# A Fourier filter feeding a squared-ReLU FFN: the last quarter of one batch's first transform moved into the first FFN group

## The chip, the cores and the metric

The kernel runs on one core of a Trainium2 chip. The metric is the device time of one execution in microseconds (us), as the median of several runs. The profile is of one further execution, and its times count from the start of that execution's span.

## The reference, cut to what matters

```python
X = np.fft.rfft(x, axis=1)                       # x: 8 batches, 3008 tokens, 256 features
Y = X * (filt_r + 1j * filt_i)[None, :, :]       # one complex factor per frequency and feature
y = np.fft.irfft(Y, n=3008, axis=1).astype(np.float32)
x = y.reshape(24064, 256)
h = np.maximum(x @ w_in, 0.0)                    # 256 -> 2048
return (h * h @ w_out).astype(np.float32)        # 2048 -> 256
```

## The kernel before, in words

The Fourier filter is four matmul stages per batch, since 3008 = 64 x 47. Stage A (`unit_a`, or `chunk_a` in the prologue) transforms over one factor and gives a tile u, which goes through DRAM to be turned (`write_u` stores a quarter of it to dU, L344; `read_u` loads the whole batch as ut, L436). Stage B (`unit_b`, L445) transforms over the other factor, and VectorE multiplies its result by the filter (L453, L460, L461, L467). Stage P (`unit_p`, L496) begins the inverse and stores to dZ; `read_z` (L514) loads it as four tiles zt; stage Y (`unit_y`, L532) finishes the inverse into yt, the FFN's input, in 16 units of 4 small matmuls.

The FFN takes groups of 512 tokens. A group has 8 slots. `ffn_g1(g, s)` (L562) makes 256 of the 2048 hidden features: 4 matmuls of 512 columns into a tile psH, which ScalarE empties with a ReLU (L566); `ffn_sq` squares the half-precision result on VectorE (L570). One group later, `ffn_g2` (L579) multiplies by W_out: 8 matmuls of 256 columns per slot, emptied by ScalarE (L590) and stored. psH has two buffers.

The order of the work is written out by hand. The main loop at L728 goes through the slots: g1 of this group, the planned work of place 0, g2 of the group before, the planned work of place 1, the output of the group before, the squaring. `fft_plan(b)` (L610) says in which slot and place each unit of batch b's filter stands. For batch 1 plan slot 0 is slot 0 of the main loop, so plan slots 0 to 7 are FFN group 0, which has no g2 of a group before it, and slots 8 to 15 are group 1. Every engine runs its instructions in this order.

Before the loop stands a prologue: the filter of batch 0 (but for Y units 4 to 15), and three quarters of stage A of batch 1: chunks 0, 2, 1 in this order (L712), stored by three `write_u` (L715). The last quarter (`unit_a` 12 to 15, chunk 3) stands in the plan, two units each in slots 8 and 9. In the plan stand too the Y units 4 to 15 of batch 0, and four casts of W_out to half precision (`cast_wout`, L333, on VectorE, slots 4, 5, 7, 7). W_out arrives in two halves by DMA (L328) into a tile of the pool p_h2, which is the buffer that group 1's hidden tile takes next.

Two small pools matter here. psF, a PSUM tile of one bank with two buffers, is used by `unit_a` and `unit_y` alike: a unit can start on TensorE when the unit two places earlier has been emptied. The pool p_u for u has three buffers; in order of use they are taken by two constants (sSPx), then u of chunk 0, 2, 1, 3. So u of chunk 3 gets the buffer of u of chunk 0, and its first writer waits until chunk 0's store to dU has completed.

The queue of the DMAs is SyncE's, in program order: zt tile 0 (two DMAs), first half of W_out, zt tile 1 (two), second half of W_out, the dU stores of chunks 0, 2, 1, zt tiles 2 and 3 (four), and later the dU store of chunk 3 and the loads of ut.

Of the kernel before, what the change touches and what calls it, by code (L numbers as in the profile page):

```python
# [110 lines left out]
def kernel(  # L111
# [9 lines left out]
    nc = tc.nc  # L121
# [35 lines left out]
    def psF(name):  # L157
        return pps.tile([128, 512], F32, tag="psF", name=name, bufs=2)
# [184 lines left out]
    def write_u(b, c):  # L343
        nc.sync.dma_start(  # L344
            out=dU[b].rearrange("(m q) d -> q m d", q=96)[:, 8 * c:8 * c + 8, :],
            in_=us.pop((b, c)))

    def unit_a(b, a):

        c, i = divmod(a, 4)  # L350
        if i == 0:
            us[(b, c)] = p_u.tile([96, 8, D], F16, tag="u", name=f"u_{b}_{c}")
        ps = psF(f"psA_{b}_{a}")
        m = slice(2 * i, 2 * i + 2)
        if b == 1:
            nc.tensor.matmul(ps[0:96, :], s1[:, c // 2, :], xw16[(b, 2 * (c % 2))][:, m, :],
                             start=True, stop=False)
            nc.tensor.matmul(ps[0:96, :], s1[0:120, 2 + c, :], xw16[(b, 1)][0:120, m, :],
                             start=False, stop=True)
        else:  # L360
            nc.tensor.matmul(ps[0:96, :], sSA, x16s[(b, c)][:, m, :], start=True, stop=True)  # L361
        o = us[(b, c)][:, 2 * i:2 * i + 2, :]
        pv = ps[0:96, :].rearrange("p (a d) -> p a d", d=D)
        if a % 2 == 0:
            nc.scalar.copy(out=o, in_=pv)  # L365
        else:
            nc.vector.tensor_copy(out=o, in_=pv)  # L367
        if i == 3:
            write_u(b, c)
# [240 lines left out]
    def fft_plan(b):  # L610

        plan = {}

        def put(r, place, f, *a):
            plan.setdefault((r, place), []).append((f, a))

        if b == 1:
            for n in range(4, 16):
                put(n if n < 8 else n + 2 if n < 12 else 2 * n - 7, n % 2, unit_y, 0, n)
            for k in range(4):  # L620
                put((4, 5, 7, 7)[k], 1, cast_wout, k, nc.vector)
        t0 = 2 if b == 1 else 6
        for a in range(12 if b == 1 else 0, 16):
            put(t0 + a // 2, a % 2, unit_a, b, a)
        put(10 if b == 1 else 14, 1, read_u, b)
        t0 = 14 if b == 1 else 19
        for p in range(12):
            r = t0 + (17 if b == 1 else 18) * p // 11
            put(r, 0, unit_b, b, p)
            put(r, 0, unit_s, b, p)  # L630
            put(r + 2, 1, unit_p, b, p)
        t0 = 34 if b == 1 else 40
        for c in range(4):
            put(t0, 1, read_z, b, c)
        if b + 1 < B:
            for c in range(2):
                put(t0 - 13, 1, load_x, b + 1, c)
            for c in range(4):
                r = t0 - 8 + 3 * c
                put(r, 1, cast_x, b + 1, c)  # L640
                if c < 2:
                    put(r, 1, load_x, b + 1, c + 2)
        for n in range(16):
            put((38 if b == 1 else 45) + n // 2, n % 2, unit_y, b, n)
        return plan
# [77 lines left out]
    for b in range(1, B):  # L723
        first = (b * S // TG) * SLOTS - (48 if b > 1 else 40)
        for (r, place), w in fft_plan(b).items():
            work[(first + r, place)] = w

    for s in range((NG + 1) * SLOTS):  # L728
        g, k = divmod(s, SLOTS)
# [40 lines left out]
```

## Time and profile before

| | |
|---|---|
| median of 3 runs | 794.04 us (793.07 to 794.68) |
| the profiled execution: its time, its span | 793.69 us, 791.9 us |
| busy: TensorE, VectorE, ScalarE, GpSimd | 778.9, 550.3, 557.4, 23.6 us |
| the chain that ended last: TensorE, VectorE, DMA, ScalarE | 89%, 6%, 3%, 1% |
| one g1 ReLU on ScalarE, one squaring on VectorE | 1024 ns, 685 ns |
| one `unit_a` emptying: ScalarE, VectorE | 572 ns, 687 ns |
| one cast of a quarter of W_out on VectorE | 682 ns |

PE is TensorE, PEld its weight loads, DVE VectorE, ACT ScalarE, POOL GpSimd, SP SyncE with its DMA queue. A line of the timeline gives the start, the length, the engine, the line of the kernel, the operation, what is written and read, how many, and in brackets how long the engine stood idle before it and what ended that. A matmul's length in the timeline has its drain in it; the chain of waits gives the spacing, 0.217 us for 512 columns.

### The profile page before, as it was taken

Reading aid. Unit: us, or ns where it says so; the run is one execution under the profiler, and the core shown is the slowest. Engines: PE = TensorE matmul, PEld = TensorE weight load, DVE = VectorE, ACT = ScalarE, POOL = GpSimd, SP = SyncE. Lnnn points to the kernel's source line nnn. Section 1 sums busy time; section 2 is a strip of 40 time slices with the busy share of each in tenths; the row PEclk is TensorE's granted clock in tenths of the full one; section 3 lists DMA queues with packets and bytes.
Section 4 is the critical chain, followed back from the end, with each engine's and each line's share of the span. In section 5 each row is a group of like instructions: output and inputs, shape, how many; then the busy total and the mean of one; then the engine's idle time right before and its main releaser. Section 6 shows DMA issues by size and latency. Waiting matters only on the chain.

```text
span 791.9 us, 14822 instructions
## 1 busy us (share of the span) xinstructions
PE 778.9 (98%) x6102; PEld 552.5 (70%) x6102; DVE 550.3 (69%) x897; ACT 557.4 (70%) x711; POOL 23.6 (3%) x36
## 2 busy tenths in 40 slices
PE   8989999999999999999999999999999999999998
PEld 5746667667676777867777676776767677676666
DVE  6866994579755897559965699556995579553342
ACT  3976776777777777767776777676777777776664
POOL 3800000000000000000000000000000000000000
PEclk9999999999999999999999999999999999999999
DMA  9994554346814557154562555424563332611111
GB/s 363 368 260 153 146 157 111 93 135 167 205 42 112 167 155 180 48 173 135 132 167 65 163 147 155 112 80 148 159 180 86 97 133 66 147 40 41 41 41 54
DMA packets 88571, 107.32 MB, mean 136 GB/s; under 512 B 6336, under 2 KB 79040, under 8 KB 84288
## 3 DMA queue, kind: packets, MB, share of 16 engines
q1 hardware_dynamic: 88296, 106.19, 46.5%
q8 instruction: 48, 0.79, 0.4%
q10 hardware_dynamic: 144, 0.18, 0.1%
q14 instruction: 19, 0.16, 0.1%
q0 software_dynamic: 64, 0.00, 0.0%
HBM read 58.12 MB, written 48.23 MB: 134 GB/s over the span
## 4 chain that ended last, share of the span: by engine, by line
PE 89%; DVE 6%; DMA 3%; ACT 1%; SPq 0%; issue 0%; DVEq 0%; ACTq 0%
PE psO L579 40%; PE psH L562 38%; PE psA L361 3%; PE psY L532 2%; PE psB L445 2%; DMA f<-in_filt_i_dram 2%; PE psP L496 2%; DVE prod L453 2%; DVE h L570 1%; DMA wout<-in_moe_w_out_dram 1%; PE psf L287 1%; PE psf L290 1%; DVE yf L467 0%; ACT sF L298 0%; DVE yf L461 0%; ACT h L566 0%
## 5 line engine op out<-in xcount | busy, mean ns | idle before, releaser
L566 ACT ACTIVATE h<-psH 128x1024 f16<-128x1024 f32 x376 | 384.9, 1024 | 189.3 <-PE psH L562 186.7
L579 PE MATMUL psO<-sWout,h 128*128 128x256 f16 x3008 | 388.9, 272 | 0.6 <-DVE h L570 0.6
L562 PE MATMUL psH<-yt,sWin 128*128 128x512 f16 (+7 forms) x1728 | 386.9, 351 | 1.6 <-DVE yt L541 0.7
L579 PEld LDWEIGHTS <-h 128*128 128x128 f16 x3008 | 290.6, 98 | 79.1 <-DVE h L570 0.9
L570 DVE TENSOR_TENSOR h<-h 128x1024 f16<-128x1024 f16 x376 | 252.6, 685 | 104.7 <-ACT h L566 104.5
L562 PEld LDWEIGHTS <-sWin 128*128 128x128 f16 x1728 | 159.5, 98 | 101.7 <-issue 3.3
L453 DVE TENSOR_TENSOR prod<-psB,sF 128x1024 f16<-128x1024 f32 x84 | 102.3, 1218 | 2.8 <-PE psB L445 2.8
L541 DVE CAST yt<-psY 128x376 f16<-128x376 f32 x62 | 34.0, 549 | 59.4 <-PE psY L532 59.4
L367 DVE CAST u<-psA 96x512 f16<-96x512 f32 x50 | 34.3, 687 | 47.3 <-PE psA L361 45.1
L498 ACT CAST ze<-psP 128x512 f16<-128x512 f32 x84 | 49.1, 585 | 17.2 <-PE psP L496 14.7
L590 ACT COPY ost<-psO 128x512 f32<-128x512 f32 (+1 forms) x96 | 55.8, 581 | 6.8 <-PE psO L579 5.3
L532 PE MATMUL psY<-sC,zt 112*128 112x94 f16 x512 | 42.4, 205 | 1.4 <-DMA zt<-dZ 1.4
L532 PEld LDWEIGHTS <-zt 112*128 112x128 f16 x512 | 35.1, 98 | 11.6 <-issue 1.6
L467 DVE TENSOR_TENSOR yf<-prod,yf 128x512 f16<-128x512 f16 x84 | 35.7, 425 | 2.9
L361 PE MATMUL psA<-x,sC 94*96 94x512 f16 x96 | 36.6, 382 | 0.0
L445 PE MATMUL psB<-ut,sSB 128*128 128x256 f16 x192 | 36.5, 273 | 0.0
L496 PE MATMUL psP<-yf,sSP 128*128 128x256 f16 x168 | 32.1, 272 | 0.5 <-DVE prod L453 0.3
L539 ACT CAST yt<-psY 128x376 f16<-128x376 f32 x66 | 30.9, 468 | 2.0 <-issue 1.7
L445 PEld LDWEIGHTS <-sSB 128*128 128x128 f16 x192 | 18.5, 98 | 19.5
L340 DVE CAST x<-x 94x2048 f16<-94x2048 f32 x24 | 29.2, 1216 | 0.0
L365 ACT CAST u<-psA 96x512 f16<-96x512 f32 x50 | 28.6, 572 | 0.0
L460 DVE COPY yf<-prod 64x512 f16<-64x512 f16 x84 | 24.3, 289 | 2.9
(65 smaller groups left out, 253.2 us busy)
## 6 DMA issues: line engine op xcount, KB each, us to landing
x<-in_x_dram SPq DMA_DIRECT2D x20, 768.0 KB
zt<-dZ SPq DMA_DIRECT2D x64, 192.0 KB
dU<-u SPq DMA_DIRECT2D x28, 384.0 KB
dZ<-ze SPq DMA_DIRECT2D x28, 384.0 KB
out_dram<-ost SPq DMA_DIRECT2D x66, 128.0 KB
out_dram<-ost SPq DMA_DIRECT2D x31, 256.0 KB
ut<-dU SPq DMA_DIRECT2D x7, 1024.0 KB
xw<-in_x_dram SPq DMA_DIRECT2D x6, 1024.0 KB
```

What stands on the lines that cost most here:

```text
L361: nc.tensor.matmul(ps[0:96, :], sSA, x16s[(b, c)][:, m, :], start=True, stop=True)
L445: nc.tensor.matmul(ps[:, i * D:(i + 1) * D], sSB[:, 2 * p + i, :], uts[b][:, 2 * p + i, :], start=True, stop=True)
L453: nc.vector.tensor_mul(out=prod, in0=ps.rearrange("p (a d) -> p a d", d=D).unsqueeze(1).to_broadcast([128, 2, 2, D]), in1=sF[:, :, 2 * p:2 ...
L467: nc.vector.tensor_add(out=yf, in0=prod[:, 0], in1=yf)
L496: nc.tensor.matmul(ps[:, i * D:(i + 1) * D], sSP[:, 2 * p + i, :], yf[:, i, :], start=True, stop=True)
L498: nc.scalar.copy(out=zes[(b, c)][:, 2 * i6:2 * i6 + 2, :], in_=ps.rearrange("p (a d) -> p a d", d=D))
L532: nc.tensor.matmul(ps[:, 94 * jj:94 * jj + 94], zt[:, 4 * (g % 2) + jj, dt * 128:(dt + 1) * 128], sSY, start=True, stop=True)
L562: nc.tensor.matmul(ps[:, i, o:o + n], sWin[:, dt, jt * 128:(jt + 1) * 128], yts[b][:, dt, r:r + n], start=(dt == 0), stop=(dt == 1))
L566: nc.scalar.activation(out=h2[:, 2 * s:2 * s + 2, :], in_=ps, func=AF.Relu)
L570: nc.vector.tensor_mul(out=v, in0=v, in1=v)
L579: nc.tensor.matmul(pso[g][:, t % 2, :], h2s[g][:, jt, t * 128:(t + 1) * 128], sWout[:, jt, :], start=(jt == 0), stop=(jt == NJT - 1))
L590: nc.scalar.copy(out=ost[:, h0:h0 + step, :], in_=pso[g][:, h0:h0 + step, :])
```

## The change

Three things move in `fft_plan(1)`, and `unit_a` changes its engine for batch 1:

- `unit_a(1, 12..15)` goes from slots 8, 8, 9, 9 to slots 1, 2, 3, 4, and with it the store of chunk 3 (slot 4). All four units are emptied by VectorE (two of them were by ScalarE).
- the four casts of W_out go from VectorE in slots 4, 5, 7, 7 to GpSimd in slots 1, 2, 4, 5.
- the Y units 8 to 11 of batch 0 go from slots 10 to 13 to slots 8 to 11.

```diff
@@ unit_a
-        if a % 2 == 0:
+        if a % 2 == 0 and b > 1:
             nc.scalar.copy(out=o, in_=pv)
         else:
             nc.vector.tensor_copy(out=o, in_=pv)
@@ fft_plan
         if b == 1:
             for n in range(4, 16):
-                put(n if n < 8 else n + 2 if n < 12 else 2 * n - 7, n % 2, unit_y, 0, n)
+                put(n if n < 12 else 2 * n - 7, n % 2, unit_y, 0, n)
             for k in range(4):
-                put((4, 5, 7, 7)[k], 1, cast_wout, k, nc.vector)
-        t0 = 2 if b == 1 else 6
+                put((1, 2, 4, 5)[k], 1, cast_wout, k, nc.gpsimd)
+        t0 = 6
         for a in range(12 if b == 1 else 0, 16):
-            put(t0 + a // 2, a % 2, unit_a, b, a)
+            put(a - 11 if b == 1 else t0 + a // 2, a % 2, unit_a, b, a)
```

VectorE's order in group 0 becomes: square of slot 0, emptying of A 12, square of slot 1, A 13, square 2, A 14, square 3, A 15, square 4, Y 5, squares 5 and 6, Y 7, square 7. TensorE's is g1 of slots 0 and 1, A 12, g1 of slot 2, A 13, g1 of slot 3, A 14, g1 of slot 4, Y 4, A 15, g1 of slot 5, Y 5 and so on.

## The prediction

> **What bounds the kernel now.** I read the chain of waits first: TensorE holds 89% of it, so a change counts where it takes matmuls out of a full TensorE or makes TensorE wait. Then I looked at the two stretches that the change touches, group 0 (49.7 to 60.6 us) and group 1 up to the first stage B unit (60.6 to 73.25), in the table of stretches (start and end, length, busy time of PE, PEld, DVE, ACT, POOL, clock, DMA share, GB/s):
>
> ```profile
> 49.70:60.60 10.90, 9.71 (x53) 4.46 (x53) 7.92 (x14) 8.40 (x10) 0.00 (x0) 1.00 1.11 313
> 60.60:73.25 12.65, 12.65 (x96) 8.51 (x95) 6.67 (x12) 8.28 (x11) 0.00 (x0) 1.00 0.42 129
> ```
>
> In group 0 TensorE has gaps, as g1 waits for ScalarE to free psH; in group 1 it is full without a gap. The A units to be moved lie in the full stretch. The timeline of TensorE and VectorE in group 0 gives the pace:
>
> ```profile
> 52.02 0.69 DVE L570 TENSOR_TENSOR h<-h 128x1024 f16<-128x1024 f16 x1 [2.00 <-ACT h L566]
> 54.17 1.02 PE L562 MATMUL psH<-yt,sWin 128*128 128x512 f16 x4 [0.20 <-ACT h L566]
> 59.16 0.54 DVE L541 CAST yt<-psY 128x376 f16<-128x376 f32 x1
> 59.76 0.81 PE L562 MATMUL psH<-yt,sWin 128*128 128x512 f16 x3 [0.50 <-DVE yt L541]
> ```
>
> The first line is the square of slot 0; after it VectorE will now meet A 12. The second is g1 of slot 4. The last two are the pivot: g1 of group 1 goes on when VectorE has emptied Y 7 (59.70), and from there TensorE is full. Third, the DMA queue, as its issues in SyncE's timeline and the rate by stretch (last column):
>
> ```profile
> 45.05 0.39 SPq L328 DMA_DIRECT2D wout<-in_moe_w_out_dram  x1
> 45.49 1.03 SPq L514 DMA_DIRECT2D zt<-dZ  x2
> 46.57 0.43 SPq L328 DMA_DIRECT2D wout<-in_moe_w_out_dram  x1
> 47.10 7.71 SPq L344 DMA_DIRECT2D dU<-u  x3
> ```
> ```profile
> 46.00:48.00 2.00, 0.55 (x4) 0.10 (x1) 0.73 (x1) 0.99 (x2) 0.00 (x0) 1.00 0.87 232
> 48.00:50.00 2.00, 1.47 (x23) 1.19 (x24) 1.08 (x2) 0.94 (x2) 0.00 (x0) 1.00 1.07 351
> 50.00:52.00 2.00, 1.74 (x8) 0.68 (x7) 0.01 (x1) 1.04 (x2) 0.00 (x0) 1.00 1.06 256
> 52.00:54.00 2.00, 1.94 (x8) 0.77 (x8) 1.39 (x2) 1.80 (x2) 0.00 (x0) 1.00 1.07 261
> 54.00:56.00 2.00, 1.83 (x12) 0.94 (x12) 1.62 (x3) 1.80 (x3) 0.00 (x0) 1.00 1.11 346
> 56.00:58.00 2.00, 1.90 (x16) 1.03 (x14) 2.00 (x5) 2.00 (x4) 0.00 (x0) 1.00 1.15 344
> ```
>
> The DMA engines are saturated from 46 to 61 us, and the store of chunk 0 (issued at 47.10) stands behind two megabytes of W_out. Its completion is the one number that decides here. Bytes: two halves of W_out (1024 KB each), zt tile 1 (2 x 192 KB) and the store itself (384 KB) are 2816 KB, or 2884 in thousands of bytes; the rates times 2 us add up from 46 us to 464, 1166, 1678, 2200, 2892 at 56.0. With a rest of zt tile 0 the last byte moves at about 56.4. The trace's semaphore events agree: the store's 16 completions come between 56.56 and 57.58.
>
> **What the Trainium skill says.** "TensorE: Matmul & The Clock Gate", Architectural detail: ScalarE and VectorE run their queues strictly in order; the timelines agree, no VectorE row leaves program order. "DMA: Bandwidth & Descriptors", Why a DMA increments its semaphore by 16 and not by 1: only the full 16 says that the data has landed, so 57.58 counts, not 56.56. "TensorE: Matmul & The Clock Gate", What's actually happening: one idle window of about 3.4 us puts the clock to half; here the clock record falls to 0.5 at 791.8, 3.3 us after the last matmul, and the longest gap before that (46.8 to 48.3) didn't do it. "SBUF — State Buffer", SBUF: two separate sides: VectorE and GpSimd share a port pair, and the loser waits; the GpSimd cast at 11.64 beside a VectorE cast took 1.56 us, against about 1.0 each for four at 35.15.
>
> **The change part by part.**
>
> *Taken out of group 1:* 8 matmuls of stage A. In the chain each takes 0.22 (0.217 exactly), so 1.73 us off a full TensorE: a gain in full. The two ScalarE emptyings (0.57 each) go too, worth nothing: ScalarE is busy 8.28 of 12.65.
>
> *Put into group 0, TensorE's part:* in slots 1 to 3 its idle time before each g1 hides 0.43 per unit, at worst 0.4 us shows; the stall below swallows it.
>
> *Put into group 0, VectorE's part, where a wait is added.* A 12's emptying is the first writer of u's buffer for chunk 3, so it waits for chunk 0's store. In the kernel before the same wait stood on ScalarE at 61.91, long after 57.58. Now VectorE reaches it at 52.7 and stands there until 57.6, with squares 1 to 3 and A 13 to A 15 behind it. Squares are not wanted before slot 8, but psF has two buffers: A 14 on TensorE needs A 12 emptied, and TensorE is in order too. So TensorE finishes g1 of slot 3 at about 54.2 and stops. Then, with 0.69 per emptying and 0.61 from one VectorE instruction to the next back to back (57.96 to 59.16 holds two squares in 1.20):
>
> - A 12 emptied 57.62 to 58.31; A 14 on TensorE 58.35 to 58.78; g1 of slot 4 to 59.65; Y 4 to 59.82.
> - VectorE: square 1 from 58.2, A 13 58.8, square 2 59.5, A 14 60.1 to 60.75. A 15 needs A 14's buffer: 60.78 to 61.21 (a second, small stall of 0.96).
> - g1 of slot 5 to 62.1, Y 5, g1 of slot 6 to 63.1, Y 6, g1 of slot 7 to 64.2, Y 7 to 64.35. ScalarE: ReLUs of slots 5 and 6 end at 63.3 and 64.3.
> - VectorE: squares 5 and 6 end at 65.0, Y 7 is emptied at 65.5. TensorE goes on at 65.55, against 59.76.
>
> So the pivot comes 5.8 us later. From there TensorE is full as before, less 1.73: the first B unit starts 4.05 us later. Stage B after it is bound by VectorE (its multiplies fill the chain from 73.7 to 113), in the same order; nothing in the chain up to the end waits for a DMA, so nothing swallows the delay.
>
> *W_out on GpSimd:* 4 casts at 1.0 (1.56 at worst). The halves land at 51.6 and 56.4, so the last ends at 58.4 (59.5 at worst), and its first users, g2 and group 1's hidden tile, come after 65. Cover: 6 us. On VectorE it saves 4 x 0.61, which the emptyings of A take again; contention for the port can hold a square behind a cast, 0 to 0.4 us. I take 0: two of the casts fall into VectorE's stall.
>
> *Y 8 to 11 sooner:* same matmuls, same engines, zt tiles 2 and 3 landed by 63.1. Nothing; 0.1 gain at most where VectorE no longer empties Y 11 just before stage B.
>
> *SyncE's queue:* the store of chunk 3 leaves at about 62 instead of 65.70 and the ut loads at about 65.3 (landing took 3.2 after the store's issue); the ut wait stands ahead of group 0's outputs, which come at 73 or later. Not on the path.
>
> Sum: +5.8 - 1.73 = +4.05. The profiled execution would become 793.69 + 4.05 = 797.7; it lies 0.35 under the median, so on the median 798.1.
>
> **The rivals.**
>
> *Forecast: the stall as worked out, 798.1.* The landing can come 0.7 sooner or later, which counts one for one, the restart 0.3: 797.1 to 799.1.
>
> *The stall also trips the clock gate.* TensorE idles from 54.2 to 58.35, 4.1 us, longer than the window that the skill names. At half speed A 14, g1 and Y 4 take 2.95 instead of 1.47, ending at 61.3: A 15 is 0.5 late. A second slow window costs up to half of 3.4 more. So +0.5 to +2.2 on the forecast; middle 799.3. For it: idle time longer than a window. Against: the windows run freely, and a gap of 4.1 covers a whole one only in some phases (0.7 of 3.4, about one in five by this estimate, somewhat more if a little work counts as idle).
>
> *The other side: the store is there in time.* If chunk 0's store is complete when VectorE reaches A 12 at 52.7, no stall arises: the emptyings of A take the place of the casts and of VectorE's idle 0.5 to 1 us waits, Y 7 is emptied at about 59.7 as before, and the 1.73 is kept: 792.3. The point from which it decides is a landing at 53.5 (57.58 less 4.05): sooner is faster. Against it stands the byte count: at 53.5 only some 2.1 of 2.9 MB have moved. That chunk 3 might take another buffer is excluded by the order in p_u: three buffers, and chunk 0 is three places earlier.
>
> *The delay is swallowed later: 794.* It would need a stretch in which TensorE and VectorE both wait for something that doesn't shift, an input load for instance. The chain after 61 us shows none.
>
> **How the numbers follow.** Forecast 0.67, clock gate 0.22, swallowed or landed by about 53.5 0.07, in time 0.04. About 0.2% (1.6 us) is what a measurement can tell from no change: slower needs 795.6 or more. Slower 0.90, same 0.06, faster 0.04. The range takes the forecast's own bounds, most of the clock case, and 1 us below for a landing sooner than I take: 796.2 to 800.0.
>
> **What would show it.** In the new trace: a VectorE idle of 4 to 5 us before the first L367, ended by the dU store; a TensorE idle of about 4 us before the L356 of A 14, and one near 1 us before A 15; the Y 7 emptying at about 65; no gap in TensorE from there to stage B, 11 us long instead of 12.65; the clock at 1.00, or 0.5 for a window in the rival. I am wrong if L367 starts before 54, or if the later batches stand less than 3 us behind those of the kernel before.

## The result and the profile after

The changed kernel takes 799.11 us (median of six executions) against 793.42 us for the kernel before, measured beside it (six). The ratio is 1.0067, with a 95% interval from 1.0053 to 1.0081: 5.3 us slower, between 4.2 and 6.4. One of the six, 1372.6 us at a mean granted clock of 0.557, is left out of the ratio. The profiled execution took 798.67 us (span 796.8), 4.98 more than that of before; times below are of profiled executions unless a median is named.

The timeline of VectorE in the changed kernel (start, length, engine, line, operation, count, and the idle time before with what ended it):

```profile
57.68 0.69 DVE L367 CAST u<-psA 96x512 f16<-96x512 f32 x1 [4.59 <-DMA dU<-u]
...
62.19 0.69 DVE L367 CAST u<-psA 96x512 f16<-96x512 f32 x1 [0.65 <-PE psA L358]
...
65.76 0.54 DVE L541 CAST yt<-psY 128x376 f16<-128x376 f32 x1
```

The square of slot 0 is done at 53.1, and then VectorE stands for 4.59 us. The first line is the emptying of A 12; its brackets name what ended the wait, a store to dU. The second is A 15, which waits for TensorE; the last is Y 7. TensorE's timeline for the same time:

```profile
53.13 1.03 PE L562 MATMUL psH<-yt,sWin 128*128 128x512 f16 x4
58.42 0.52 PE L356 MATMUL psA<-xw,sC 128*96 128x512 f16 x1 [4.26 <-DVE u L367]
...
59.16 1.91 PE L562 MATMUL psH<-yt,sWin 128*128 128x512 f16 x4
...
61.99 1.03 PE L562 MATMUL psH<-yt,sWin 128*128 128x512 f16 x4
...
66.35 0.81 PE L562 MATMUL psH<-yt,sWin 128*128 128x512 f16 x3 [0.45 <-DVE yt L541]
...
78.10 0.38 PE L445 MATMUL psB<-ut,sSB 128*128 128x256 f16 x2
```

TensorE idles for 4.26 us before A 14, because A 14 needs the PSUM buffer that VectorE hasn't emptied. Then comes something that the profile of the kernel before doesn't have: g1 of slot 4 takes 1.91 us, that of slot 5 again 1.03. The table of stretches gives the reason in its third column from the end, the granted clock:

```profile
58.00:60.00 2.00, 1.58 (x4) 0.56 (x4) 2.00 (x4) 0.00 (x0) 0.60 (x1) 0.63 1.11 372
60.00:62.00 2.00, 2.00 (x10) 0.97 (x9) 1.54 (x3) 0.89 (x1) 0.00 (x0) 0.51 0.50 139
...
67.00:78.10 11.10, 11.10 (x89) 7.72 (x88) 4.98 (x9) 7.34 (x9) 0.00 (x0) 1.00 0.45 165
```

From 58.53 to 61.94 TensorE runs at half speed. The last row is the gain: from the end of the pivot's three matmuls to the first unit of stage B TensorE is full, and this takes 11.10 us. In the kernel before the same stretch, with the 8 matmuls of stage A in it, takes 12.85:

```profile
60.40:73.25 12.85, 12.85 (x97) 8.63 (x96) 6.87 (x12) 8.28 (x11) 0.00 (x0) 1.00 0.43 131
```

The pivot (the 66.35 line) is 6.59 later than before (59.76), the first B unit 4.85 later (78.10 against 73.25). From there to the end the difference stays: the ReLUs of the last groups start 4.86 later.

The chain of waits of the changed kernel tells the same in one piece (start, length, what):

```profile
47.46 10.10 DMA dU<-u
...
57.68 0.70 DVE u L367
...
58.42 0.52 PE psA L356
...
65.84 0.47 DVE yt L541
...
66.35 0.81 PE psH L562 x3
```

A store of 384 KB is now a part of the chain that sets the end; the chain of the kernel before has no such store in this stretch.

### The profile page after: what moved, and what is told of

Its sections match the earlier page's. It is cut to its first block, busy times and chain, and to the rows that moved or that the text cites. A ratio compares the mean times of both kernels' runs of the same rounds, so it can differ in the third digit from the quotient of the medians.

```text
span 796.8 us, 14814 instructions
## 1 busy us (share of the span) xinstructions
PE 780.6 (98%) x6102; PEld 553.1 (69%) x6102; DVE 550.4 (69%) x895; ACT 556.7 (70%) x709; POOL 28.1 (4%) x40
## 4 chain that ended last, share of the span: by engine, by line
PE 92%; DVE 4%; DMA 2%; ACT 1%; SPq 0%; issue 0%; ACTq 0%; DVEq 0%
PE psO L579 40%; PE psH L562 39%; PE psA L361 3%; PE psY L532 3%; PE psB L445 2%; PE psP L496 2%; DMA dU<-u 1%; DVE prod L453 1%; PE warm L268 1%; DVE h L570 1%; PE psf L287 1%; PE psf L290 1%; ACT sF L298 0%; ACT h L566 0%; DVE yf L467 0%; DVE prods L453 0%
```

## The experiments

My theory: the loss is one wait, A 12's emptying on VectorE for the completion of a dU store, which stops VectorE and through psF TensorE; a half-speed window after it adds to it; the casts and the Y units cost next to nothing. The rivals: the casts on GpSimd slow VectorE's squares; the Y units' new places cost; or the A units in group 0 cost without any stall. Experiments are given as edits to the changed kernel, where not said otherwise. Each median is given with that of the kernel before, measured beside it, and the ratio with its interval.

### Another buffer for the moved chunk (x1_other_buffer)

```diff
-            us[(b, c)] = p_u.tile([96, 8, D], F16, tag="u", name=f"u_{b}_{c}")
+            pool, tag = (p_x16, "x16") if b == 1 else (p_u, "u")
+            us[(b, c)] = pool.tile([96, 8, D], F16, tag=tag, name=f"u_{b}_{c}")
```

> The changed kernel, but u of chunk 3 of batch 1 lies in a free buffer of the pool p_x16, so that its first emptying has no store to wait for; all else as changed. Theory (the wait for the store of chunk 0 is the whole loss): no VectorE wait before L368, no 4 us gap on TensorE, clock 1.00 throughout, and the 1.73 us of stage A stay gained: 793.4 - 1.7 = 791.7. Rival (the four emptyings on VectorE and the casts on GpSimd crowd group 0 by themselves): Y 7 is emptied 1 us or more later than in the kernel before, 793.5 to 795.

Measured: 793.57 (13 executions) against 793.57; ratio 1.0000 (0.9991 to 1.0008). In its profile the wait and the half-speed window are gone, and its median is that of the kernel before. VectorE of this kernel in group 0 (all line numbers after L352 are one higher here):

```profile
52.48 0.68 DVE L368 CAST u<-psA 96x512 f16<-96x512 f32 x1
53.08 0.92 DVE L571 TENSOR_TENSOR h<-h 128x1024 f16<-128x1024 f16 x1
53.92 0.68 DVE L368 CAST u<-psA 96x512 f16<-96x512 f32 x1
...
60.29 0.54 DVE L542 CAST yt<-psY 128x376 f16<-128x376 f32 x1
```

So the stall is the cause of the loss. But the kernel isn't faster than the one before either: the pivot comes at 60.89 instead of 59.76, 1.13 later, and eats most of the 1.73; the 0.60 that is left in this profile doesn't show in the median. VectorE is busy almost without a gap from 51.87 on (the longest is 0.15), and the squares that start beside a GpSimd cast (51.93 to 54.90 and 56.46 to 58.99) take 0.75 to 0.92 instead of 0.68.

### The store ahead of W_out (x2_store_first)

```diff
     read_z(0, 0)
-    load_wout(0)
     read_z(0, 1)
-    load_wout(1)
     for c in (0, 2, 1):
         chunk_a(1, c)
-    for c in (0, 2, 1):
+        if c == 0:
+            write_u(1, c)
+    load_wout(0)
+    load_wout(1)
+    for c in (2, 1):
         write_u(1, c)
```

Chunk 0 is stored as soon as it is made, and W_out is loaded after it.

> The changed kernel with its buffers as they are, but the store of chunk 0 is issued ahead of both halves of W_out (and right after chunk 0 is made). Theory (it is the store's place in the DMA queue that sets the stall): the store lands near 51, before VectorE reaches A 12 at 52, no stall, about 791.7 to 792.5; W_out lands some 2 us later, which its users at 60 and later don't see. Rival (the wait is for something else than this store, or its landing hangs on fixed latency): stall as before, about 799.

Measured: 793.66 (13) against 793.57; ratio 1.0002 (0.9993 to 1.001). The store lands at 51.23, before VectorE comes to A 12 (52.03), so there is no stall: the same wait, met by an earlier landing, costs nothing. The gain that I expected didn't come. W_out now arrives later, the casts fall at 54.53 to 57.01 and 57.53 to 60.01, and two squares beside the second pair take 2.62 (in x5_a_only, with no cast on GpSimd, two in a row take 1.28):

```profile
57.94 2.62 DVE L570 TENSOR_TENSOR h<-h 128x1024 f16<-128x1024 f16 x2
```

Y 7 stands behind these squares (60.48), and TensorE waits 1.49 for it at the pivot (61.07).

### TensorE kept busy in the stall (x3_fill_stall)

Fourteen matmuls of zeros into an unused PSUM tile stand after g1 of slot 3. They change nothing in what is waited for, only whether TensorE works meanwhile.

```diff
     run(work, s, 0)
+        if s == 3:
+            pf = psO("fill").rearrange("p a d -> p (a d)")
+            for _ in range(14):
+                nc.tensor.matmul(pf, zero, sF[:, 0, 0:2, :], start=True, stop=True)
```

> The changed kernel with 14 matmuls of zeros (512 columns, into a free PSUM tile that nobody reads) in the stall after g1 of slot 3, so that TensorE does not idle for 4 us; the wait itself stays. Theory (the clock gate adds about 1 us to the stall): clock 1.00, stage A 14 and g1 of slot 4 at full speed, 0.6 to 1.0 faster than the changed kernel: about 798.2. Rival (the slow window is hidden behind VectorE's pace): clock 1.00 and the same time, 799.0.

Measured: 797.84 (5) against 793.57; ratio 1.0054 (1.0041 to 1.0068); mean clock 0.999 to 1.0, against 0.995 to 0.997 for the changed kernel. TensorE's timeline:

```profile
53.74 3.19 PE L735 MATMUL fill<-sF,zero 128*128 128x512 f16 x14
58.17 0.38 PE L356 MATMUL psA<-xw,sC 128*96 128x512 f16 x1 [1.24 <-DVE u L367]
...
58.60 1.03 PE L562 MATMUL psH<-yt,sWin 128*128 128x512 f16 x4
...
65.51 0.81 PE L562 MATMUL psH<-yt,sWin 128*128 128x512 f16 x3 [0.45 <-DVE yt L541]
```

The stall is the same (VectorE waits 4.64 us, to 57.42), g1 of slot 4 is back at 1.03, and the execution took 3.99 us more than that of before. That is the stall without the window. From A 12's emptying to the pivot it takes 8.09 (57.42 to 65.51), in the changed kernel 8.67 (57.68 to 66.35): the window cost 0.58 in that execution. By the medians it is about 1.1 (798.97, the changed kernel's five that count, less 797.84), but these were measured on two occasions, and two of the five had lower mean clocks (0.996 and 0.995) than the profiled one, so perhaps more than one window.

### One part of the change at a time

Only the A units, on the kernel before (x5_a_only): casts and Y units stay where they were.

```diff
-        if a % 2 == 0:
+        if a % 2 == 0 and b > 1:
...
-        t0 = 2 if b == 1 else 6
+        t0 = 6
-            put(t0 + a // 2, a % 2, unit_a, b, a)
+            put(a - 11 if b == 1 else t0 + a // 2, a % 2, unit_a, b, a)
```

> The kernel before with stage A 12 to 15 moved to slots 1 to 4 and emptied by VectorE, but with W_out still cast by VectorE in slots 4, 5, 7, 7 and the Y units where they were. Theory (the move alone makes the stall; the casts then stand behind it on VectorE, two of them ahead of Y 7): the stall in full and about 1.2 more: 799.5 to 800.5. Rival (the stall needs the casts on GpSimd or the Y units moved): about 793.5.

Measured: 798.67 (4) against 793.75; ratio 1.0061 (1.0046 to 1.0076). The A units alone, with their emptying on VectorE, make the stall:

```profile
58.09 0.69 DVE L367 CAST u<-psA 96x512 f16<-96x512 f32 x1 [4.61 <-DMA dU<-u]
```

I expected 0.8 to 1.8 more, for the casts on VectorE behind the stall. They cost less: from A 12's emptying to the pivot it is 8.26 (58.09 to 66.35), with the clock full after the stall, against 8.09 in x3_fill_stall, so 0.17.

Only the casts, on the kernel before (x4_casts_only):

```diff
-                put((4, 5, 7, 7)[k], 1, cast_wout, k, nc.vector)
+                put((1, 2, 4, 5)[k], 1, cast_wout, k, nc.gpsimd)
```

> The kernel before with one part of the change alone: the four casts of W_out on GpSimd, in slots 1, 2, 4, 5. Theory (harmless and slightly useful): Y 7 is emptied earlier, the 0.50 us gap of TensorE ahead of it shrinks: 792.9 to 793.4. Rival (the shared port holds the squares behind GpSimd's casts): 793.5 to 795.

Measured: 794.03 (13) against 793.57; ratio 1.0005 (0.9997 to 1.0013), no difference that can be told by the ratio. A small loss shows when executions of like clock are set side by side: twelve of the 13 had a mean clock of 0.999 or 1.0, with a median of 794.01, against 793.48 for the 26 such ones of the kernel before. So the rival's figure came true and not the theory's. The profile has the mechanism. VectorE and GpSimd:

```profile
57.31 2.28 DVE L570 TENSOR_TENSOR h<-h 128x1024 f16<-128x1024 f16 x2
```
```profile
56.34 2.71 POOL L333 CAST sWout<-wout 128x1024 f16<-128x1024 f32 x2 [2.24 <-DMA wout<-in_moe_w_out_dram]
```

The pair of squares at 57.31 lies beside the casts from 56.34 to 59.05 and takes 2.28, not 1.28. So the 2.4 us that VectorE no longer spends on casting buy nothing: the pivot is at 60.11, against 59.76, and the execution took 0.34 more.

Only the Y units, on the kernel before (x10_y_only):

```diff
-                put(n if n < 8 else n + 2 if n < 12 else 2 * n - 7, n % 2, unit_y, 0, n)
+                put(n if n < 12 else 2 * n - 7, n % 2, unit_y, 0, n)
```

> The kernel before with one part of the change alone: the Y units 8 to 11 of batch 0 in slots 8 to 11. Theory (same matmuls in a full TensorE): no change, 793.4 to 793.6, at most 0.1 faster. Rival (with stage A still in slots 8 and 9, two more units per slot wait for psF, which has two buffers): 793.8 to 795.

Measured: 795.83 (7) against 793.75; ratio 1.0031 (1.0018 to 1.0043). I expected no change, and this is a loss of its own:

```profile
62.44 0.33 PE L532 MATMUL psY<-sC,zt 112*128 112x94 f16 x4 [2.33 <-DMA zt<-dZ]
```

Y 8 in slot 8 needs zt tile 2, which lands at 62.3, and TensorE waits 2.33 us for it. In the changed kernel slot 8 comes at 67, when the tile (61.13) has long been there: the stall hides this wait.

### The Y units back, with the other buffer (x11_buffer_y_back)

The edit is that of the first experiment and the reverse of the last diff.

> The kernel with the other buffer, and the Y units 8 to 11 back in slots 10 to 13; stage A in slots 1 to 4 on VectorE and the casts on GpSimd as in the changed kernel. Theory (without the stall, Y 8 in slot 8 comes to zt tile 2 just as it lands, between 61.1 and 62.3, so part of the executions wait for it; this hides the gain of the kernel with the other buffer): Y 8 never waits, 792.7 to 793.2, some 0.5 faster than with Y sooner. Rival (Y's place does nothing once stage A is out of slots 8 and 9): the same as with the other buffer alone, 793.6.

Measured: 793.98 (13) against 793.81; ratio 0.9996 (0.9988 to 1.0004). Without the stall the Y units' place makes no difference that can be told, and in x1's profile Y 8 runs at 61.53 without a wait for its tile; in x10's it was due at about 60.1.

### Which store is waited for, and what its time is worth

The stores in another order (x9_store_later):

```diff
-    for c in (0, 2, 1):
+    for c in (2, 1, 0):
```

> The changed kernel, but of the three dU stores that of chunk 0 is issued last (order 2, 1, 0 instead of 0, 2, 1). Theory (the stall lasts until this store has landed): it lands near 59.7 instead of 57.6, everything behind it comes 2.1 later, and a second slow clock window may add up to 1.7: 801.0 to 802.7. Rival (the stall ends with something else, the second half of W_out at 56.5 for instance): 799.0 as before.

Measured: 797.98 (4) against 793.75; ratio 1.0055 (1.0043 to 1.0068). Neither expectation held:

```profile
57.39 0.69 DVE L367 CAST u<-psA 96x512 f16<-96x512 f32 x1 [5.16 <-DMA dU<-u]
```

The wait ended just after the first store had landed (57.26), and this was now chunk 2's. So chunk 3 doesn't take chunk 0's buffer by its place in the order of use; as far as these two orders show, it takes the buffer of the chunk whose store is issued first.

All three stores behind zt tiles 2 and 3 (x13_store_after_z):

```diff
+    for c in range(2, 4):
+        read_z(0, c)
     for c in (0, 2, 1):
         write_u(1, c)
...
-    for c in range(2, 4):
-        read_z(0, c)
```

> The changed kernel, but zt tiles 2 and 3 (four loads of 192 KB) are issued ahead of the three dU stores, so that chunk 0's store has 0.79 MB more in front of it. Theory (the loss follows the landing of the first store one for one): it lands near 59.9 instead of 57.6, the first emptying of A 12 starts then, and everything comes 2.3 later: 801.0 to 802.5, more if a further clock window is slow. Rival (the loss does not hang on the store's place in the queue): 799.0 as before.

Measured: 802.58 (4) against 793.81; ratio 1.0108 (1.0095 to 1.0122). The first store lands at 61.41, 1.5 later than I had worked out from the bytes ahead of it (59.9):

```profile
61.53 0.69 DVE L367 CAST u<-psA 96x512 f16<-96x512 f32 x1 [7.84 <-DMA dU<-u]
```

A landing 3.85 later than in the changed kernel (57.56) puts the pivot 4.29 later (70.64) and the median 3.5 to 3.6 higher (from 799.11 or 798.97). The landing is passed on about one for one, as the theory has it.

### Can the move pay at all?

The squares of group 0 are wanted only by g2 in group 1. In x1's variant with squares later (y1_squares_later) they stand behind the emptyings:

```diff
-        if g < NG:
+        if g == 0:
+            for j in ((), (), (), (0,), (1,), (2,), (3,), (4, 5, 6, 7))[k]:
+                ffn_sq(0, j)
+        elif g < NG:
```

> Chunk 3 in the other buffer (no store to wait for), and in group 0 the squares come later on VectorE: squares 0 to 3 in slots 3 to 6, squares 4 to 7 after the emptying of Y 7 in slot 7. Theory (what ate the 1.73 us in the kernel with the other buffer is VectorE's backlog ahead of Y 7, made of squares that the GpSimd casts stretch to 0.75 to 0.92 us, and of a 0.41 us wait of stage A 15): g1 of group 1 goes on after Y 7 at about 59.9 instead of 60.9, 792.0 to 792.6, faster than the kernel before. Rival (ScalarE's ReLUs set the pace in group 0, whatever VectorE does): the pivot stays at 60.5 or later, 793.3 to 793.6.

Measured: 793.85 (14) against 793.81; ratio 0.9996 (0.9989 to 1.0004). Missed. The second pair of casts (56.42 to 59.27) still stretches squares, one at 56.63 to 1.53, and TensorE waits 1.02 for Y 7 at the pivot (60.92).

In the next (y2_all) the Y units are back and only two casts are on GpSimd; the other two are on VectorE in slot 7, behind Y 7; the squares are later still.

```diff
-                put((1, 2, 4, 5)[k], 1, cast_wout, k, nc.gpsimd)
+                put((1, 2, 7, 7)[k], 1, cast_wout, k, nc.gpsimd if k < 2 else nc.vector)
...
+            for j in ((), (), (), (0,), (), (1,), (2,), (3, 4, 5, 6, 7))[k]:
```

> The other buffer, Y 8 to 11 back in slots 10 to 13, the first two casts on GpSimd and the last two on VectorE after the emptying of Y 7, and squares 3 to 7 of group 0 after that too. Theory (VectorE then has nothing stretched or queued ahead of Y 7, and the 1.73 us of stage A are kept but for what TensorE and ScalarE themselves lose in slots 1 to 4): TensorE goes on after Y 7 at 59.6 to 60.0, B 0 starts near 71.8 instead of 73.2: 792.0 to 792.6, faster than the kernel before. Rival (ScalarE's pace in group 0 eats it): 793.2 to 793.6.

Measured: 794.81 (13); ratio 1.0002 (0.9994 to 1.001). Missed again: of the wait for Y 7 only about 0.15 is left, but five squares in slot 7 come too late for g2, which waits for them at 63.36 and 65.77. The profile also has a half-speed window at the start of group 0 (49.72 to 53.14), and the times fall in two heaps: 793.2 to 793.7 at a mean clock of 1.0, and 794.8 to 795.1 at 0.998, which is seven of the 13. The kernel before shows the same two heaps (about 793.0 to 794.1, and 794.7 to 795.5, about a third of its executions), so that a median alone says little here.

The last (y3_squares_spread) differs from this by the squares alone:

```diff
-            for j in ((), (), (), (0,), (), (1,), (2,), (3, 4, 5, 6, 7))[k]:
+            for j in ((), (), (0,), (1,), (2,), (), (3,), (4, 5, 6, 7))[k]:
```

> As the kernel with the other buffer, Y back and the last two casts on VectorE after Y 7, but the squares of group 0 are spread: one each in slots 2, 3, 4 and 6, four after the casts in slot 7, so that g2 of group 0 doesn't wait for squares as it did there (0.2 to 0.6 us twice). Theory (TensorE and ScalarE between them have only about 0.2 us of free time per slot in group 0, since a slot takes 1.07 and g1 0.87, so that four A units of 0.43 cost 0.9 to 1.0 there and only 0.7 to 0.8 of the 1.73 is kept): TensorE goes on after Y 7 some 0.9 later than in the kernel before, 792.7 to 793.0 where the clock stays at 1.00. Rival (the idle time of group 0 takes all of stage A once nothing else is in the way): 791.9 to 792.2.

Measured: 792.88 (21) against 793.56; ratio 0.9992 (0.9985 to 0.9999). It is the fastest kernel of the study, by 0.1%, with an interval that just ends below 1. Heap by heap it is clearer: 792.74 against 793.39 at a mean clock of 0.999 or 1.0, and 794.22 against 794.86 below that, so 0.65 and 0.64. TensorE:

```profile
59.76 1.18 PE L563 MATMUL psH<-yt,sWin 128*128 128x512 f16 x4 [0.27 <-ACT yt L540]
...
62.51 1.02 PE L580 MATMUL psO<-sWout,h 128*128 128x256 f16 x6
63.74 0.39 PE L580 MATMUL psO<-sWout,h 128*128 128x256 f16 x2 [0.21 <-DVE h L571]
...
72.47 0.38 PE L446 MATMUL psB<-ut,sSB 128*128 128x256 f16 x2
```

The pivot stands where it stood before the change, but for one matmul (0.22) that the kernel before had already done. Of the 1.73 this leaves 1.51. Of that Y 7 takes 0.14: its emptying ends at 60.08, and the second of the four matmuls from 59.76 waits for it, so that g2 starts at 60.77. The squares of slots 4 to 7 take 0.57: from 62.51 to 63.74 six matmuls take that much more than the 0.66 that they need. The first B unit comes 0.78 sooner than in the kernel before, and so does the end. The time was forecast rightly (792.7 to 793.0), but by luck: I had the loss in group 0, with a pivot 0.9 later, where the A units cost only these 0.22 and 0.14, and the larger part, 0.57, went to squares that came late.

## Why the prediction was right, and where it was not

*The stall: right.* A 12's emptying was put at 57.62 and came at 57.68, A 14 at 58.35 and 58.42. The store's completion was at 57.58 then and 57.56 now. The other buffer, the earlier store and the later store show it as the cause: taken away, the loss is gone; later by 3.85, the pivot moves by 4.29.

*The gain: right.* The full stretch before stage B is shorter by 12.85 - 11.10 = 1.75, or by 6.59 - 4.85 = 1.74; 1.73 was forecast.

*Nothing swallows it: right.* +4.85 at the first B unit, +4.86 at the last ReLUs.

*The pivot: mis-sized, +6.59 and not +5.8.* The predicted 65.55 is 0.80 short of 66.35. Of this 0.06 is the start of A 12's emptying; 0.58 is the half-speed window (8.67 against 8.09 in the kernel whose TensorE was kept busy); the remaining 0.16 is the restart itself at full speed (8.09 against my 7.93), in which one square beside a cast took 0.83 instead of 0.68. My sum was rounded: 65.55 less 59.76 less 1.73 is 4.06, not 4.05; with the 0.80 it is 4.86, against 4.85. The kernel whose TensorE was kept busy is the forecast's own case, a stall at a full clock, and it took 797.84; 798.1 was forecast.

*The clock gate: mechanism named, chance too low.* I gave it 0.22 as a rival, by the argument that an idle time of 4.1 us covers a whole window of 3.4 in one phase of five. The profiled execution, at a mean clock of 0.997, had the window; the other four that count had 0.995 to 0.997, and as one window takes 0.002 off the mean (half of 3.41 us in 797), each of them had at least one, behind the stall or elsewhere. "TensorE: Matmul & The Clock Gate", What's actually happening, says that the window is free-running and that a warm clock falls after an idle one. The traces agree: the half speed lasts 3.41 us here, and in x13_store_after_z the clock changes at 49.55, 52.96, 59.79 and 66.61, one, two and two times 3.41 apart. They don't agree with my reading of "idle" as no work at all. The 3.41 us ahead of the half speed (55.11 to 58.53) have 0.11 of matmul in them, and the windows at the start of group 0 follow stretches with far more (the last section). So the true forecast was the stall with the gate; my price for it (+0.5 to +2.2) holds the 0.58 and the 1.1. It is also why the result lies at the upper part of the range: the forecast that I held likelier, with its own bounds, ended at 799.1.

*The casts at "0": right for the changed kernel, for a reason of place alone.* On its own the move of the casts gains nothing and costs 0.3 to 0.5 (x4_casts_only); without the stall it is one of two things that hold x1 back. "SBUF — State Buffer", SBUF: two separate sides, says that a VectorE operation with two inputs in SBUF competes with a GpSimd operation that reads SBUF, and that the loser waits for the whole instruction. The traces agree, and show the distinction: the squares (two inputs in SBUF) go from 0.68 to 0.75 to 1.53, the emptyings between them (one input, in PSUM) stay at 0.67 to 0.69. The longest stretch, 0.85, is less than one cast (1.04), so none of them shows a wait for a whole one. I had read the passage and taken the case of two casts for the price.

*"Y 8 to 11 sooner: nothing": false by itself.* Alone it costs 2.1 us by the median (2.33 of waiting in the profile). I compared the landing with the late slot of the stalled kernel, which holds only as long as the stall does.

*The rival "in time", 792.3: the size was wrong.* When the wait is taken away the kernel gives 793.6. I let group 0 hide the 0.43 of each A unit and took the casts' removal as room on VectorE. In x1 the slots with an A unit are 1.29 to 1.30 apart (g1 at 51.89, 53.18, 54.48), and VectorE has no gap; the pivot moves by 1.13.

*"Chunk 3 takes chunk 0's buffer, in order of use": imprecise.* It takes the buffer whose store is issued first. Here both are chunk 0, so that the number was right.

What stays open: where the half-speed windows lay in the four executions without a trace, and so how the medians' +5.3 divides beyond the profile's +4.98. Two of them had a lower mean clock than the profiled one (0.995 and 0.996), so probably more of such windows. Nor did any run move the A units and leave A 12 and A 14 to ScalarE, as in the kernel before; whether ScalarE would then have stood in VectorE's place is not shown.

## What to carry to other kernels

Before work is moved earlier, look at who frees the buffer that it writes: an instruction whose buffer is read by a DMA in flight inherits that DMA's place in the queue, and the landing can be worked out from the bytes ahead of it (57.6 and 51 came out as 57.56 and 51.23, but 59.9 as 61.41). In an engine that works strictly in order, the wait costs everything behind it, and with two PSUM buffers it stops TensorE two units later. A gap of over 4 us on TensorE should be priced with a half-speed window after it, and a part that costs nothing beside a stall has to be priced again for the kernel without it.

## What the runs showed of the hardware

- *Half-speed windows without a long gap.* The kernel before has no idle time over 1.5 us on TensorE at the start of group 0, only light work from 46.5 to 49.5, and about a third of its executions have a mean clock of 0.997 or 0.998 and take 1.4 to 1.6 us more. The profile of y2_all shows such a window, with eight matmuls of g1 in 3.51 us (2.03 in the kernel before). My remark in the prediction that the gap from 46.8 to 48.3 didn't lower the clock holds for that one profile only:

```profile
49.52 3.51 PE L563 MATMUL psH<-yt,sWin 128*128 128x512 f16 x8 [0.28 <-ACT yt L540]
```

- *A little work doesn't keep the clock up.* The clock changed only at steps of 3.41 us, so the time can be cut at those steps and the matmul work in the 3.41 us ahead of each half-speed window counted. After the long gaps it was, by the profile, 0.11 us (the changed kernel), 0.06 (x9) and 0.00 (x13). Ahead of the windows at the start of group 0 it was 1.57 (x5), 1.64 (y2) and 1.71 (x13), where most of the matmuls are the small ones of stage Y and its zeros.
- *A gap of 2.67 us did nothing.* In the profile of x5 the early window came, the stall absorbed its delay, and the gap before A 14 was 2.67 us. A step of the clock at 57.08 divides it, and the emptier of the two stretches still has 1.63 us of mostly wide matmuls; after it the clock was 1.00. With 1.65 in x2 and 1.68 in x3 it stayed full as well. So the busy time alone doesn't draw the line, and no run here measured what does. Back to full the clock came each time only after 3.41 us at half speed in which TensorE was busy for 3.27 or more: in x9 and x13 it stayed at half for a second window, after 2.51 and 0.92 us of matmul in the first.
- *The price of one window varies.* It was 0.58 us by profiles behind the stall, and 1.4 to 1.6 between the heaps of the kernel before, whose mean clocks are one window's worth apart.
- *The completions of one store are spread.* The 16 completions of the first dU store (384 KB) come over 1.03 us (56.53 to 57.56), so that it landed a microsecond after its first completion (0.78 in x10, 1.71 in x2).
